# Loading Q weights ahead of K, wider Q/K matmuls, smaller weight pieces and an on-chip mask in a fused transformer block

## Chip, cores, metric

One core of a Trainium2 chip runs the whole program. The metric is device time in microseconds (us) of one execution; each kernel is run several times, and a profile is taken of one run. TensorE is called PE, VectorE DVE, ScalarE ACT, GpSimd POOL and SyncE SP, as in the profile; "PEld" is PE's weight load. The trace records the clock that PE was granted: 1.0 is full speed.

## The reference, cut to what matters

Two pre-normalized layers on 2,048 tokens of width 448: sliding, dilated attention (16 heads of 28, 8 keys per query at distance 2), then a mixer and an MLP.

```python
qkv = _layernorm(x) @ wqkv                    # 448 x 1344
idx = pos[:, None] - jnp.arange(8)[None] * 2  # 8 keys per token
attn = softmax(where(idx >= 0, q . k[idx] * scale, -1e9))
h = x + (attn . v[idx]) @ wo
# the second layer works on _layernorm(h):
# gelu(ln @ w1), shifted by 1 or 2 tokens, @ w2; then gelu(ln @ w3) @ w4   (w3: 448 x 1792)
```

## The kernel before: the parts concerned

Tokens are split by parity (index `a`), since the distance is 2: each parity is a sequence of 1,024, and `u` numbers its quarters of 256. HT holds the normalized activations, transposed. Its 448 rows do not fill 128-row tiles, so pairs of 64-row matmuls share PE's array ("r64"): in the trace of the changed kernel such a pair takes 216 ns with 512 columns, as one 128-row matmul of 512 columns does, and 109 with 256 (medians of the distances between starts).

The program is a list of operations with dependencies. A scheduler written in Python, inside the kernel file, replays that list with modelled durations and fixes the order of every engine before anything is compiled. Its constants are therefore part of the kernel, and so is a table of priorities (`rank`).

```python
LEAD = 600.0        # bulk DMAs may be issued this long before the queue runs dry (ns)
FETCH = 2900.0      # modelled time to fetch 256 PE instructions

def setup():
    load_x(0); load_x(1)
    wload("wqk", wst, A_wqkv[:, 0:2 * D], ("sp", "sp"))   # Q and K together, 4 transfers
    load_x(2); load_x(3)
    # ... constants; WARM = 36 dummy matmuls of 512 columns, lowest priority, wherever PE is free

def wqk_copies():                     # repacks the weights, 8 copies on ACT or DVE
    for c in range(4):
        for w in range(2): ...        # w = 0: Q, w = 1: K

def loads_b():
    dma("msk", msk[half[1], 1, :], msk[half[0], 1, :], 64 * 912, after=first)
    dve("tensor_copy", 280, out=msk[:, 0, :], in_=msk[:, 1, :])

def phase_QK(u):                      # u = 0..3
    for c in range(4):                # one tile: Q and K of 4 heads, 2 parities, 256 columns
        for w in range(2):
            for b in range(7):
                for a in range(2): ins.append(mm(... HT[r, b, 16+256*u : 16+256*u+256] ...))
        copy(QK[...], T(...), 1024)
# [cut: V, attention, WO, LN2, W1, W2, LN3, W3, W4]
```

## Time and profile before

| quantity | value | how to read it |
|---|---|---|
| three runs | 207.03, 207.33, 208.37 us | median 207.33 |
| profiled run | 209.0 us, span 207.2 | a slow run of this kernel; a second trace was taken later |
| PE busy | 92% of the span | PE is the bound, so its gaps and its clock matter |
| first Q/K matmul | 13.19 us | PE waits for weights until here |
| last matmul | 201.85 us | 5.4 us of stores follow |
| mean clock | 0.983 | two stretches of 3.41 us at half clock |

The prediction shows and explains the lines.

### The profile page before, as it was taken

How to read it: one execution, taken by the hardware profiler on the slowest of the kernel's cores; microseconds unless marked ns; L12 is line 12 of the kernel's file. 1: busy time of each engine (PE TensorE's matmuls, PEld its weight loads, DVE VectorE, ACT ScalarE, POOL GpSimd, SP SyncE). 2: the span in 40 equal slices, each digit the busy share in tenths (PEclk: the TensorE clock that was granted, in tenths of full speed). 3: DMA queues.
4: the chain of work that ended last, by engine and by line, in shares of the span. 5: the costliest groups of instructions: out<-in, count | busy, mean ns of one | idle time of the engine just before them, and what ended most of it. 6: DMA issues, size and time to landing. Idle time of an engine off the chain costs nothing.

```text
span 207.2 us, 7398 instructions
## 1 busy us (share of the span) xinstructions
PE 191.5 (92%) x3391; PEld 129.7 (63%) x3391; DVE 112.2 (54%) x261; ACT 101.8 (49%) x107; POOL 48.2 (23%) x90
## 2 busy tenths in 40 slices
PE   7859998996999999599999999999999999999990
PEld 2437765774756785446888555688895558855540
DVE  7569955442479908969990299990005920022221
ACT  2346699585349999950766900076672006700000
POOL 6311510000004500370850028770000730000000
PEclk9999999998899999979999999999999999999999
DMA  5996596654467500050252002561000231001111
GB/s 169 303 295 130 124 144 182 223 203 134 147 172 156 117 12 6 3 93 0 49 95 44 0 3 47 134 109 26 0 3 3 44 89 47 3 0 44 44 44 52
DMA packets 29610, 18.11 MB, mean 87 GB/s; under 512 B 21192, under 2 KB 28680, under 8 KB 29576
## 3 DMA queue, kind: packets, MB, share of 16 engines
q1 hardware_dynamic: 29576, 17.61, 34.1%
q8 instruction: 27, 0.44, 0.9%
q14 instruction: 7, 0.06, 0.1%
HBM read 10.67 MB, written 1.84 MB: 60 GB/s over the span
## 4 chain that ended last, share of the span: by engine, by line
PE 77%; DMA 7%; DVE 6%; ACT 3%; issue 3%; SPq 1%; POOL 1%
PE ps L1354 77%; DMA h<-in_A_wqkv_dram 4%; DMA HT<-ln 2%; DVE xin L1354 1%; ACT lnz L1354 1%; ACT pt L1354 1%; DVE pt L1354 1%; SPq L1354 1%; DVE st L1354 1%; DVE xb L1354 1%; DVE ln L1354 1%; POOL rstd L1354 1%; ACT QK L1354 0%; DVE arena L1354 0%; DVE mv L1354 0%
## 5 line engine op out<-in xcount | busy, mean ns | idle before, releaser
L1354 PE MATMUL ps<-HT,w_s 64*128 64x256 bf16 (+1 forms) x1064 | 56.0, 264 | 0.2 <-DMA HT<-ln 0.2
L1354 PEld LDWEIGHTS ps<-HT,w_s 64*128 64x128 bf16 x1064 | 49.5, 94 | 6.9 <-issue 1.1
L1354 DVE TENSOR_TENSOR xb<-ps,xb 128x448 bf16<-128x448 f32 (+1 forms) x24 | 18.4, 774 | 58.8 <-PE ps L1354 58.7
L1354 POOL TENSOR_SCALAR vtmp<-mv 128x2 f32<-128x2 f32 x32 | 6.2, 193 | 111.9 <-DVE mv L1354 110.5
L1354 ACT ACTIVATE arena<-ps 128x1024 bf16<-128x1024 f32 x14 | 14.3, 1024 | 36.1 <-PE ps L1354 36.1
L1354 PE MATMUL ps<-HT,arena 64*128 64x256 bf16 x448 | 28.1, 280 | 3.3 <-DVE arena L1354 2.3
L1354 ACT ACTIVATE QK<-ps 128x1024 bf16<-128x1024 f32 (+2 forms) x23 | 21.6, 948 | 14.2 <-PE ps L1354 14.1
L1354 PEld LDWEIGHTS ps<-HT,arena 64*128 64x128 bf16 x448 | 22.5, 98 | 8.6 <-issue 4.6
L1354 POOL TENSOR_TENSOR rstd<-vtmp,mhalf 128x2 f32<-128x2 f32 x32 | 22.5, 702 | 2.7
L1354 PE MATMUL ps<-w_s,h 128*128 128x448 bf16 x112 | 21.9, 352 | 0.2 <-issue 0.2
L1354 PE MATMUL ps<-w_s,arena 128*128 128x448 bf16 x112 | 21.5, 352 | 0.0
L1354 ACT ACTIVATE h<-ps 128x1024 bf16<-128x1024 f32 x14 | 14.3, 1024 | 12.5 <-PE ps L1354 12.5
L1354 DVE BATCH_NORM_STATS2 st<-xin 128x6 f32<-128x448 bf16 x32 | 18.4, 607 | 0.4 <-DMA xin<-in_A_x_dram 0.4
L1354 PEld LDWEIGHTS ps<-w_s,arena 128*128 128x128 bf16 x112 | 11.0, 98 | 10.2
L1354 PEld LDWEIGHTS ps<-w_s,h 128*128 128x128 bf16 x112 | 10.8, 98 | 10.3 <-issue 0.4
L1354 POOL TENSOR_TENSOR xb<-xb,xin 128x448 bf16<-128x448 bf16 x16 | 16.1, 1035 | 4.0 <-DVE ln L1354 4.0
L1354 ACT ACTIVATE pt<-ps 128x912 bf16<-128x912 f32 x18 | 15.7, 930 | 0.9 <-PE ps L1354 0.6
L1354 DVE TENSOR_SCALAR ln<-xin,mv,rstd 128x448 bf16<-128x448 bf16 x32 | 14.4, 496 | 2.4 <-POOL rstd L1354 2.1
L1354 DVE TENSOR_TENSOR QK<-ps,lnz 128x456 bf16<-128x456 f32 (+1 forms) x24 | 11.2, 505 | 6.1 <-PE ps L1354 5.9
L1354 PE MATMUL ps<-wv_s,HT 64*64 64x448 bf16 x252 | 14.2, 376 | 0.0
L1354 DVE TENSOR_TENSOR pt<-pt,msk 128x912 bf16<-128x912 bf16 x18 | 11.1, 628 | 4.7 <-ACT pt L1354 4.6
L1354 PE MATMUL ps<-wo_s,QK 128*128 128x448 bf16 x64 | 12.9, 358 | 0.0
(53 smaller groups left out, 167.8 us busy)
## 6 DMA issues: line engine op xcount, KB each, us to landing
w_s<-in_B_w_dram SPq DMA_DIRECT2D x6, 448.0 KB, 3.4
w_s<-in_B_w_dram SPq DMA_DIRECT2D x9, 224.0 KB, 2.9
xin<-in_A_x_dram SPq DMA_DIRECT2D x8, 224.0 KB, 7.9
out_dram<-xb SPq DMA_DIRECT2D x8, 224.0 KB, 1.9
h<-in_A_wqkv_dram SPq DMA_DIRECT2D x2, 672.0 KB, 6.0
wv_s<-in_A_wqkv_dram SPq DMA_DIRECT2D x2, 336.0 KB, 6.1
w_s<-in_B_w_dram SPq DMA_DIRECT2D x2, 336.0 KB, 3.4
wo_s<-in_A_wo_dram SPq DMA_DIRECT2D x4, 98.0 KB
```

The source lines that it names most:

```text
L1354: inst = getattr(eng, meth)(**kw)
```

## The change

The intent: let the Q part of the projection start while K's weights are still coming; shorten the list of PE instructions in the attention part; issue bulk weights in smaller pieces with less of a queue; keep the mask off the DMA queue. The scheduler's constants and priorities were fitted anew, so that the order of many operations differs.

```diff
-    LEAD = 600.0
+    LEAD = -300.0
-    FETCH = 2900.0
+    FETCH = 3400.0
-            fe[2] = at + self.FETCH + min(3600.0, 0.7 * max(0.0, qfree - at))
+            fe[2] = at + self.FETCH + min(1000.0, 0.5 * max(0.0, qfree - at))
 # [cut: modelled DMA rates 320 -> 300 and 200 -> 100]
-        wload("wqk", wst, A_wqkv[:, 0:2 * D], ("sp", "sp"))
+        for w in range(2):
+            wload("wqk%d" % w, wst[:, :, D * w:D * w + D], A_wqkv[:, D * w:D * w + D], ("sp", "sp"))
 # wqk_copies: the loops over c and w change places (all of Q first)
-        dma("msk", msk[half[1], 1, :], msk[half[0], 1, :], 64 * 912, after=first)
-        dve("tensor_copy", 280, out=msk[:, 0, :], in_=msk[:, 1, :])
+        for k in (1, 0):
+            dve("tensor_copy", 280, out=msk[half[1], k, :], in_=msk[half[0], 1, :])
+        dve("tensor_copy", 280, out=msk[half[0], 0, :], in_=msk[half[0], 1, :])
-        wload("w3", w3_s, B_w3, ..., each=True)
+        for k in range(2):
+            wload("w3_%d" % k, w3_s[:, :, 896 * k:896 * k + 896], B_w3[:, 896 * k:896 * k + 896], ..., each=True)
 # phase_QK(u) becomes phase_QK(u, nu) with 256*nu columns, and a tile holds Q or K, not both:
-    phase_QK(0) ... phase_QK(1) ... phase_QK(2) ... phase_QK(3)
+    phase_QK(0, 1) ... phase_QK(1, 1) ... phase_QK(2, 2)
 # [cut: a new table of priorities]
```

## The prediction

> **What bounds the kernel now.** I read first the busy shares, then the slices, then the chain that ended last, then TensorE's (PE's) timeline, and last the stretches where PE's clock or its idle time stood out.
>
> ```profile
> PE 191.5 (92%) x3391; PEld 129.7 (63%) x3391; DVE 112.2 (54%) x261; ACT 101.8 (49%) x107; POOL 48.2 (23%) x90
> PE   7859998996999999599999999999999999999990
> PEclk9999999998899999979999999999999999999999
> PE 77%; DMA 7%; DVE 6%; ACT 3%; issue 3%; SPq 1%; POOL 1%
> q8 instruction: 27, 0.44, 0.9%
> ```
>
> PE is 92% busy and makes 77% of the chain. It has three parts: until 13.2 us it waits for inputs, from 13.2 to 202.0 us it runs nearly without a gap, and a 5 us tail stores the last rows. So only four things can shorten the span: an earlier start, less PE work, fewer PE gaps, fewer slow-clock stretches. The start, from the chain in order of time:
>
> ```profile
> 2.71 0.55 SPq L1354
> 3.27 0.04 issue
> 3.31 9.02 DMA h<-in_A_wqkv_dram
> 12.33 0.02 issue
> 12.36 0.70 DVE arena L1354 x2
> 13.05 0.14 issue
> 13.19 1.71 PE ps L1354 x28
> ```
>
> The Q and K weights land together at 12.33; two repacking copies follow, then the first Q/K matmul at 13.19. The other operand, HT, was ready at 10.50 (ACT's two copies: from 8.53, 1.97 us). The gaps, from PE's timeline:
>
> ```profile
> 36.31 0.28 PE L1354 MATMUL ps<-pt,vt 64*32 64x57 bf16 x23 [0.81 <-issue]
> 40.44 1.25 PE L1354 MATMUL ps<-HT,arena 64*128 64x256 bf16 x19 [0.29 <-issue]
> 49.48 0.30 PE L1354 MATMUL ps<-pt,vt 64*32 64x57 bf16 x28 [1.49 <-issue]
> ...
> 83.61 0.23 PE L1354 MATMUL ps<-pt,vt 64*32 64x57 bf16 x11 [0.40 <-issue]
> ...
> 85.72 0.31 PE L1354 MATMUL ps<-QK 28*64 28x57 bf16 x13 [0.63 <-ACT lnz L1354]
> 87.17 0.34 PE L1354 MATMUL ps<-QK 28*64 28x57 bf16 x19 [1.15 <-issue]
> ```
>
> "issue" means that PE waited for nothing the profile knows, and always in the middle of a run of identical small matmuls. Counting matmuls up to each: 604 before the first, 731 before the second, 986 before the third: spacings of 128 or (nearly) a multiple of it. Each matmul is a load and a multiply, so 128 are 256 instructions. These are waits for instruction fetch: 0.44 MB in 27 transfers is 16 KB each, 256 instructions of 64 bytes. They sum to 0.81 + 0.29 + 1.49 + 0.40 + 1.15 = 4.14 us. And busy time and clock by stretch:
>
> ```profile
> 36.50:50.00 13.50, 11.13 (x416) 8.46 (x395) 5.92 (x9) 10.13 (x11) 0.00 (x0) 1.00 0.59 199
> 50.00:60.00 10.00, 10.00 (x164) 6.96 (x161) 4.24 (x6) 3.89 (x5) 0.00 (x0) 0.83 0.45 127
> 76.00:88.00 12.00, 9.78 (x462) 6.65 (x460) 9.58 (x19) 11.19 (x14) 1.57 (x4) 0.98 0.01 4
> 88.00:97.00 9.00, 9.00 (x66) 4.17 (x56) 7.03 (x13) 2.70 (x3) 4.20 (x5) 0.84 0.31 54
> ```
>
> (Columns: stretch, length, busy of PE, PEld, DVE, ACT, POOL, PE clock, DMA share, GB/s.) Each stretch with fetch gaps is followed by one with a mean clock of 0.83 or 0.84. The trace's clock record has exactly two half-rate pieces in the body, 49.94 to 53.36 and 87.49 to 90.90, right behind the 1.49 and 1.15 us gaps. 84 QK matmuls there take 6.42 us instead of 4.76. Half of 3.41 us is lost in each: 3.4 us in all.
>
> [...] PE was about half busy, not idle, in the window ahead of each (1.85 us in the first). [...] here a block took 3.56 us boundary to boundary with idle queues (83.61 to 87.17) and 4.13 with weights loading (36.31 to 40.44).
>
> **The change part by part.** The instruction order of the changed kernel can be listed without running it, and I cut both into blocks of 128 matmuls (after the first 93).
>
> *Start.* Q comes as 784 KB ahead of K's 784 KB, each in four transfers instead of four for both. In the old kernel 1,568 KB landed between about 3.5 us (x there, DVE begins at 3.42) and 12.33. Half of that time is 4.4 us, so Q by 7.9; rows of 896 bytes instead of 1,792 make twice the packets, so I take 8.6 to 9.4 (an estimate). HT is then the later operand: on DVE the first Q copy (0.38) stands ahead of the second pair of normalizations, and ACT does a Q copy (0.85) before the HT copies. From Q at 9.0: copy to 9.4, normalize 0.97 to 10.4, transposes 0.56, HT copy 0.92, so PE starts near 11.9 to 12.0, against 13.19. The mask copies on DVE (3 x 0.25 us and two memsets) lie in front of Q's landing and are free; the mask's DMA of 57 KB goes. K (estimated 12.5 to 13.5) has 56 Q matmuls, 3.3 us, to hide behind. Part of the gain could be lost at the next tokens' transposes, since their statistics now stand behind K's copies on DVE. Net: -1.0.
>
> *PE work.* 224 matmuls of 256 columns become 112 of 512. Today 28 of them need 1.63 us start to start (31.74 to 33.37), 58 ns each; the weights' 308 ran at 55.2. With 512 columns the fixed part is paid half as often: about 108 each. 224 x 57.5 - 112 x 107.5 = 0.84. -0.8. The columns streamed do not change, so no more is to be had. ACT and DVE still evacuate 16 tiles of 1,024 elements.
>
> *Fetch.* 112 matmuls fewer is 0.875 of a block, so about one fetch fewer, and the order is reshuffled. Pure work per block, at durations from the timeline (57-column 10 ns, 448-column 49 or 189, warm-up fillers 216), in the critical part:
> old, from matmul 349: 4.7, 2.6, 3.8, 3.6, 2.8, 5.3 us; later (76 to 88 us): 2.9, 2.9, 1.5
> new, from matmul 349: 3.7, 3.4, 3.1, 3.2, 4.5, 8.3 us; later: 3.8, 2.6, 7.2
> [...] With 3.9 us under load the new early blocks lose 0.2 + 0.5 + 0.8 + 0.7 = 2.2, and the 2.6 block about 1.0 at 3.6: 3.2 against 4.14. [...] the worst old case, 1.49, fell among the 448 KB pieces. -1.0, with 1.2 either way.
>
> *Clock.* The 1.5 us block and its neighbours are gone, and no two new blocks are so short that half a window stands empty. I give each slow window two chances in three of vanishing: 2 x 1.7 x 0.65 = -2.2.
>
> *New waits.* Between the second W2 group and the first W3 matmul the new order has 10.6 us of PE work; in the old trace the path from W2's end (82.4) to the landed transposes (93.7) took 11.3. +0.3 to +0.5. ACT's table loads fall from six to four, 2 x 1.28 us, but late, where ACT waits for PE: nothing. The tail is unchanged.
>
> Sum: -1.0 - 0.8 - 1.0 - 2.2 + 0.4 = -4.6, and 207.3 becomes 202.7.
>
> **Rivals.** (a) The early start is eaten: PE arrives sooner at attention but is held by ACT's softmax chain or the later transposes, and only work and clock pay. For: ACT is busy 9.10 of 9.50 us in 27 to 36.5, and 11.19 of 12 in 76 to 88. Against: data waits there are about 1 us in all and ACT is not full in between. Then about 204. (b) Fetch stays the bound: evenly short blocks of 3.1 to 3.4 us all stall if contention makes the period 4.5 to 5, as happened once. That is 4 x 1.3 us, no gain, perhaps one slow window left: 205 to 206. For: the bulk loads move into the same stretch. Against: smaller pieces. (c) All goes well: no slow window, fetch waits of 1.5 us, start at 11.5: -1.6 - 0.8 - 2.6 - 3.4 = -8.4, so 199.
>
> **Range and chances.** Clock and fetch each carry an uncertainty of a good microsecond and are linked[...]. I take 199.8 to 205.6. The 2% line is at 203.2, half a microsecond above my value, so it is little better than even: 0.57 faster, 0.41 within 2%, 0.02 slower, since nothing in the change adds PE work.
>
> **What would show it.** Right: the first Q/K matmul near 12 us; 112 matmuls of 512 columns at 107 to 110 ns; "issue" gaps that sum to about 3 us, none over 1.2; no slice under 9 in the clock row of the body; the rest of PE's stream unchanged. Wrong: a start at 13 or later (Q not ahead, or HT held by the copies), a new DMA wait ahead of W3, slow windows still there, or an ACT or DVE wait of over 1 us in attention.

## The result, and the profile after

The changed kernel took 200.88 us (median of 4 runs, 200.41 to 201.24) against 207.85 (4 runs, 207.03 to 208.87) in the same rounds. The ratio is 0.9661, interval 0.9608 to 0.9715: faster. Ratios here are the record's: fast runs of one kernel over fast runs of the other in the same rounds. They are not quite the ratio of the medians, nor of the means over all the runs listed. The time lies in the predicted range, on its fast side.

First the page of the changed kernel: engine totals, two rows of the slices, the chain by engine.

```profile
PE 186.8 (94%) x3275; PEld 123.0 (62%) x3279; DVE 111.0 (56%) x262; ACT 99.3 (50%) x106; POOL 48.3 (24%) x90
PE   7599999899999999999899999999999999999990
PEclk9999999999999999999999999999999999999999
PE 70%; DVE 12%; ACT 9%; POOL 3%; DMA 2%; issue 2%; POOLq 0%
```

The clock row has no digit under 9 any more, and the only slices of PE under 8 are the first two and the last. DMA fell from 7% to 2% of the chain: the weights no longer release the start. Next, PE's timeline of the same run, four lines: the first Q/K matmuls, the one fetch gap left, the new wait ahead of the later W1 matmuls, and the end.

```profile
11.35 6.29 PE L1360 MATMUL ps<-HT,arena 64*128 64x256 bf16 x112
...
38.88 0.82 PE L1360 MATMUL ps<-HT,arena 64*128 64x512 bf16 x5 [0.82 <-issue]
...
98.33 3.23 PE L1360 MATMUL ps<-HT,w_s 64*128 64x256 bf16 x56 [0.50 <-DMA HT<-ln]
...
193.46 0.16 PE L1360 MATMUL ps<-ones,fbit 128*1 128x1 bf16 x1
```

This trace has three more "issue" gaps, 0.16, 0.25 and 0.16 us, in the attention part. They are not waits: beside each the list of instructions has one more warm-up matmul of 216 ns than the trace records (this trace has 3,275 matmuls, those of e0_changed and e0c, of the same kernel, 3,279). Such a gap has to be counted against the program before it is read as a stall.

The same four stretches as before, with the same columns:

```profile
36.50:50.00 13.50, 12.43 (x378) 6.28 (x378) 6.92 (x11) 11.40 (x14) 0.00 (x0) 1.00 0.32 88
50.00:60.00 10.00, 10.00 (x180) 5.38 (x182) 9.27 (x21) 6.97 (x9) 2.64 (x6) 1.00 0.51 117
76.00:88.00 12.00, 11.09 (x311) 6.27 (x310) 11.97 (x24) 6.12 (x9) 6.13 (x8) 1.00 0.51 123
88.00:97.00 9.00, 8.96 (x197) 8.88 (x196) 8.95 (x28) 7.88 (x8) 3.72 (x9) 1.00 0.60 84
```

PE is busy 1.3 us more in each of the first and third stretch, and the clock is 1.00 in all four. (These are the same times, not the same work, since the order differs.)

The first profile of the kernel before was a slow run, so it must not be held against a fast one. A second trace of it, fast (206.94 us, span 205.2; run e8_before below), has these waits of PE:

```profile
12.41 5.07 PE L1354 MATMUL ps<-HT,arena 64*128 64x256 bf16 x84 [1.62 <-DVE arena L1354]
...
40.29 1.25 PE L1354 MATMUL ps<-HT,arena 64*128 64x256 bf16 x19 [0.84 <-issue]
...
49.33 0.30 PE L1354 MATMUL ps<-pt,vt 64*32 64x57 bf16 x28 [1.49 <-issue]
...
81.63 0.23 PE L1354 MATMUL ps<-pt,vt 64*32 64x57 bf16 x11 [0.37 <-issue]
...
84.91 0.34 PE L1354 MATMUL ps<-QK 28*64 28x57 bf16 x19 [0.87 <-issue]
```

Start 12.41, fetch gaps 0.84 + 1.49 + 0.37 + 0.87 = 3.57 us, one slow clock window in the body (85.67 to 89.08). Against a fast trace of the changed kernel (run e0_changed, span 198.6, start 11.44, last matmul 193.24, fetch gap 0.64) the 6.6 us between the spans come out so: start 1.0; fetch 2.9; half of one slow window 1.7 (in the first trace the 84 matmuls under one took 6.42 us, in e8_before the same 84 at full clock 4.76); the remaining 1.0 is data waits (1.6 us in the old stream, 1.4 in the new one), the tail and what is too small to name.

### The profile page after: what moved, and what is told of

It reads as the page before. It is cut to its first block, busy times and chain, and to the rows that moved or that the text cites. A ratio compares the mean times of both kernels' runs of the same rounds, so it can differ in the third digit from the quotient of the medians.

```text
span 199.1 us, 7188 instructions
## 1 busy us (share of the span) xinstructions
PE 186.8 (94%) x3275; PEld 123.0 (62%) x3279; DVE 111.0 (56%) x262; ACT 99.3 (50%) x106; POOL 48.3 (24%) x90
## 4 chain that ended last, share of the span: by engine, by line
PE 70%; DVE 12%; ACT 9%; POOL 3%; DMA 2%; issue 2%; POOLq 0%
PE ps L1360 70%; ACT QK L1360 3%; ACT pt L1360 3%; DVE st L1360 2%; DVE ln L1360 2%; DVE xin L1360 2%; DVE QK L1360 2%; ACT lnz L1360 2%; DMA HT<-ln 2%; DVE xb L1360 2%; DVE pt L1360 1%; ACT L1356 1%; POOL wo_s L1360 1%; POOL rstd L1360 1%; POOL msk L1360 1%
## 5 line engine op out<-in xcount | busy, mean ns | idle before, releaser
L1360 PEld LDWEIGHTS ps<-HT,w_s 64*128 64x128 bf16 x1064 | 50.6, 94 | 6.2 <-issue 1.1
L1360 ACT ACTIVATE QK<-ps 128x1024 bf16<-128x1024 f32 (+2 forms) x24 | 22.5, 951 | 15.1 <-PE ps L1360 15.1
L1360 PE MATMUL ps<-HT,arena 64*128 64x256 bf16 (+1 forms) x336 | 26.5, 305 | 1.2 <-issue 0.8
L1360 PEld LDWEIGHTS ps<-HT,arena 64*128 64x128 bf16 x336 | 15.6, 94 | 9.5 <-issue 1.9
L1360 PEld LDWEIGHTS ps<-w_s,arena 128*128 128x128 bf16 x112 | 10.9, 98 | 10.2
L1360 POOL TENSOR_TENSOR xb<-xb,xin 128x448 bf16<-128x448 bf16 x16 | 16.6, 1068 | 0.2 <-DVE ln L1360 0.2
L1360 PE MATMUL ps<-w_s,QK 112*128 112x448 bf16 x64 | 13.0, 353 | 0.0
L1360 PE MATMUL ps<-wv_s,HT 64*64 64x448 bf16 x252 | 12.7, 351 | 0.1
```

Source lines behind the costliest of these rows:

```text
L1360: inst = getattr(eng, meth)(**kw)
```

## The experiments

For each experiment on the changed kernel, its order was computed first, and the edit was made on the finished order. So an edit moves nothing else. Differences are of means, in us, against the changed kernel on the same chip; the intervals of the ratios to the kernel before are 0.35 to 1.2% to either side, since that kernel itself scatters by up to 2.5%. The changed kernel scatters by up to 0.7%. Worked out from the runs listed, the 95% intervals of the differences are about 1.0 us to either side for e1, 0.9 for e1c and e3, 1.3 for e2, 1.2 for e9 and 0.4 for e5c. So the +0.80 of e3 alone is not clear of noise.

| run | edit | median us | ratio to before | against the changed kernel |
|---|---|---|---|---|
| e0_changed, e0c | none | 200.42, 200.70 | 0.9688, 0.9731 | (200.61 and 200.69 mean) |
| e1_one_load, e1c | Q and K in one load | 201.40, 201.43 | 0.9717, 0.9784 | +0.95, +1.03 |
| e2_cols256 | 256 columns again | 202.09 | 0.9750 | +1.50 |
| e3_big_pieces | w3 in 8 pieces again | 201.32 | 0.9723 | +0.80 |
| e9_order_only | all three undone | 203.73 | 0.9884 | +3.5 (+3.2 without the profiled run) |
| e7_small_fillers | 12 fillers shortened | 201.46 | 0.9699 | other chip |
| e5_ht_first, e5c | HT first, mask copies later | 199.43, 199.50 | 0.9634, 0.9674 | -1.23 (e5c) |
| e8_before | the kernel before | 207.08 | 0.9985 | |
| e6_before_shift64 | before, 64 tiny matmuls more | 207.61 | 0.9998 | |

**The yardstick.** Two sets of the unchanged new kernel.

> The changed kernel once more, so that the next three have it on their own chip. All theories: 200.4 to 201.3 us, no slow clock window in the body, one instruction-fetch gap of about 0.8 us near 38 us.

> The changed kernel as the yardstick for the next three on one chip: 200.3 to 201.2 us, gap of 0.6 to 0.9 us near 38 us.

Both came out as expected: means of 200.61 and 200.69, no slow window in the body of either trace. e0c's fetch gap was 1.01 us, a little more than expected.

**One load for Q and K.**

```diff
     q, k = S.qk_loads[:4], S.qk_loads[4:]
+    for o, kw in zip(q, whole_width): o.ins = [("dma_start", kw)]   # Q's transfers fetch Q and K
+    # K's transfers are dropped; normalizations and HT copies go ahead of the repacking on DVE and ACT
```

> The changed kernel with Q and K weights in one set of four transfers again, and the order on DVE and ACT that suits it (normalizations and HT copies ahead of the repacking); everything else in the same order. Theory (start passes on in full): first Q/K matmul back at 13.0 to 13.4 us instead of 11.35, time 1.6 to 2.0 us over the changed kernel, 202.4 to 203.0. Rival (early start is eaten by later waits): within 0.4 us of the changed kernel.

> One load for Q and K again, once more, as its first set of runs lay 1.0 us over the changed kernel while its trace said 2.0 at the start. Theory (full passing, the load's landing varies between runs): first Q/K matmul between 12.4 and 13.5, time over the changed kernel by what the trace shows of the start, within 0.5 us. Rival (half of it is absorbed by later waits): 1.0 us over whatever the start says.

The first set was 0.95 us over the changed kernel, against an expected 1.6 to 2.0. Its trace started Q/K at 13.46, 2.0 later than the yardstick's, but that was the slowest of its six runs (202.67; the others 200.57 to 202.22). So the set was repeated: +1.03, now with a trace of a more usual run (201.22, median 201.43).

```profile
12.49 6.29 PE L1411 MATMUL ps<-HT,arena 64*128 64x256 bf16 x112 [1.09 <-DVE arena L1411]
```

12.49 is 0.97 later than e0c's 11.52, and the mean time 1.03 more. The traces show where the start goes: PE reaches the fetch gap near 38 us 2.00 us later than the yardstick in e1 and 1.02 in e1c, so up to there the start passes on in full. From there the gap itself differs between runs (0.64 to 1.01 us in the yardsticks), and the last matmul comes 2.28 and 0.44 us later. What had misled me was the landing of the single load, which differs between runs by about a microsecond (11.34 to 12.33, and Q/K starts at 12.41 to 13.46, in the six traces that have it).

**256 columns again.**

```diff
-  mm(out[:, 0:512], lhsT, rhs[:, 0:512], start, stop)
+  mm(out[:, 0:256], lhsT, rhs[:, 0:256], start, False); mm(out[:, 256:512], lhsT, rhs[:, 256:512], False, stop)
```

> The changed kernel with each 512-column Q/K matmul cut into two of 256 columns, all else in the same order: 112 matmuls more. Theory A (fewer instructions to fetch): blocks of 128 matmuls of 2.6, 2.8, 2.7, 2.9 and 2.6 us appear, fetch gaps sum to 3 to 5 us instead of 0.8, 203.5 to 206.5 us, perhaps with a slow window. Theory B (fixed cost per matmul, as I predicted it): 0.8 us more and no new gap, 201.7. Theory C (only the new order matters): 201.0.

1.50 us more. The fetch gaps of its trace:

```profile
39.34 1.27 PE L1400 MATMUL ps<-HT,arena 64*128 64x256 bf16 x19 [1.33 <-issue]
...
47.01 0.30 PE L1400 MATMUL ps<-pt,vt 64*32 64x57 bf16 x28 [0.99 <-issue]
...
82.36 0.58 PE L1400 MATMUL ps<-QK 28*64 28x57 bf16 x47 [0.56 <-issue]
```

2.88 us against 0.64: new gaps, as theory A had it, though smaller than its 3 to 5, and the time fell short of its 203.5. (Q/K also started 0.51 us later in this trace than in e0_changed, which the edit does not explain.) The matmuls themselves decide against theory B. The longest run of them in each kernel:

```profile
47.24 3.23 PE L1400 MATMUL ps<-HT,arena 64*128 64x256 bf16 x56
```

```profile
45.62 3.20 PE L1360 MATMUL ps<-HT,arena 64*128 64x512 bf16 x28
```

56 of 256 columns take 3.23 us, 28 of 512 take 3.20. That is 0.03 us for 28 of the wide ones, about 0.1 us for all 112. From one pair of 64-row matmuls to the next it is 109 ns with 256 columns and 216 with 512 (medians in e0_changed), so a wide pair saves 2 ns and the 56 wide pairs 0.1 us. The wide matmuls pay off because they are fewer instructions, hardly because they run faster.

**Larger weight pieces.** Each pair of w3 transfers is fetched as one, in the place of its first.

```diff
-  16 transfers: 12 of 224 KB, 4 of 112 KB (column halves of w3, one half after the other)
+  8 transfers: 6 of 448 KB, 2 of 224 KB (all columns)
```

> The changed kernel with w3 in 8 transfers of the old sizes (448 and 112 KB) instead of 16, each in the place of the first of its pair. Theory (a fetch waits behind bulk transfers, smaller pieces shorten that): gaps in 30 to 60 us grow by 0.5 to 1.5 us in sum, 201.4 to 202.4. Rival (sizes don't matter, the pacing or the order does): within 0.3 us of the changed kernel.

(The 112 KB in the expectation is a slip: the small pieces have 224 KB, as in the diff.) 0.80 us more, inside the theory's range, but not for its reason, and with an interval that reaches zero. The gap near 38 us was 0.86, no more than in the yardsticks (0.64 to 1.01). A new wait stands at the first W3 matmul:

```profile
89.53 2.69 PE L1416 MATMUL ps<-HT,w_s 64*128 64x256 bf16 x46 [1.07 <-DMA w_s<-in_B_w_dram]
```

With all columns in every piece, the first W3 group waits for the last piece; in the changed kernel it needs the first column half alone, and no such wait exists (that half had landed by 69.05 us in e0_changed; here the last piece landed at 89.49). The wait of 0.54 at the later W1 is gone in exchange, so 0.53 us of it remains. So cutting w3 by columns helps the start of W3 in this order. That piece size matters to instruction fetch is not shown by this run; the size was changed without changing the pacing, and pacing by itself was not tried.

**The order alone.**

> The changed kernel's order and on-chip mask alone: one load for Q and K, 256 columns, w3 in 8 pieces. Theory (parts add): 1.0 + 1.5 + 0.8 over the changed kernel, 203.9 us (203.2 to 204.6), so that the new order is worth some 3 us against 207.4, with fetch gaps of 2.5 to 3.5 us still there, but no gap over 1.4 and at most one slow clock window in the body. Rival (order is worth nothing, the parts do it all): 206.5 to 208, two slow windows.

All three edits at once: 203.73 median; the parts add up (0.99 + 1.50 + 0.80 = 3.3, measured 3.5 over all six runs, which are all fast, or 3.2 without the profiled one). Against the kernel before, 0.9884 remains (0.9828 to 0.9940; within 2%, so classed as the same, but clear of 1): the new order and the on-chip mask are worth some 2.4 us (0.0116 of 206; the interval says 1.2 to 3.5, and all six runs listed give 2.0). "Order" here includes the pacing of the loads and the tiles that hold Q or K alone, which this run keeps too. Its fetch gaps sum to 1.82 us (1.56 + 0.26), less than the 2.5 to 3.5 expected. How this order still suffers is seen at 40.91, in its slowest run, the profiled one:

```profile
40.91 1.97 PE L1447 MATMUL ps<-HT,arena 64*128 64x256 bf16 x19 [1.56 <-issue]
42.81 0.94 PE L1447 MATMUL ps<-QK 28*64 28x57 bf16 x64
43.68 2.20 PE L1447 MATMUL ps<-HT,arena 64*128 64x256 bf16 x28
```

The gap is larger than I had allowed (1.56, not under 1.4). The clock record goes to half from 41.32 to 44.73, right behind it: 19 matmuls need 1.97 us there, 1.27 in e2_cols256, which had the same instructions, a gap of 1.33 and no slow window.

**Are the gaps instruction fetch?** The kernel before, untouched, and with 64 matmuls of 32 columns added where PE waits for the weights anyway:

```diff
+    last_warm_up.ins += [matmul(out[:, 0:32], same weights, rhs[:, 0:32])] * 64
```

> The kernel before once more, because its first profile fell in a slow run (209.0 us, its others 207.0 to 208.4). All theories: 206.5 to 208 us. Theory (fetch gaps follow from the instruction count): the issue gaps stand at the same matmuls (about 604, 731, 986, 1880, 2010) and sum to 3 to 4.5 us; one or two slow clock windows in the body. Rival (gaps are chance of that run): other places.

> The kernel before with 64 matmuls of 32 columns added while TensorE waits for the Q/K weights, nothing else. Theory (instruction fetch in blocks of 128 matmuls): every gap moves 64 matmuls towards the start of the stream. Old gaps at 604, 731, 986 are gone; new ones near 411 and 667 (inside runs of 57-column Q/K matmuls), near 923, and 1819 and 1947 of the old count. Blocks of 2.6, 2.1, 3.1, 2.8 and 1.6 us against a period of 3.6 to 4.1: gaps of about 1.2, 1.7, 0.7, 0.8 and 1.9, 6.3 in sum instead of 4.1, time 1 to 3 us over the kernel before. Rival (gaps belong to certain data or buffers): same places, same time.

Untouched, four of the five old gaps stand at the same matmuls; the one at 604 was absent. With 64 more, all old places are clean (the profiled run is a slow one, 207.73 us, so its gaps are read for their places first), and:

```profile
38.16 0.38 PE L1387 MATMUL ps<-QK 28*64 28x57 bf16 x23 [1.47 <-issue]
...
47.66 1.27 PE L1387 MATMUL ps<-HT,arena 64*128 64x256 bf16 x20 [0.78 <-issue]
...
85.00 0.60 PE L1387 MATMUL ps<-pt,vt 64*32 64x57 bf16 x51 [1.00 <-issue]
```

The first is in the middle of a run of Q/K products, after the 668th matmul of the old count (expected near 667), the second after the 922nd (923), the third 13 records into the run in which 1947 lies. Counted from the start of the stream with the 64 included, they stand at 732, 986 and 2007, where the untouched kernel has gaps at 731, 986 and 2007 (a trace misses a few matmuls); the changed kernel's one gap is at 731 too. So the gaps belong to instruction number, not to data.

That they are fetch can be seen in the DMA records of the same traces, which list each 16 KB instruction transfer: 27 in the first trace, where PE executes 6,782 instructions, and 26 in the trace of the result, with 6,554. In all 14 traces, 25 "issue" gaps of 0.29 us or more stand before 90 us, and each ends 1.07 to 1.53 us after such a transfer has landed. With idle queues (83.6 us in the first trace of the kernel before; DMA share 0.01 from 76 to 88) the transfer of the next block began 1.1 us after PE had entered a block, took 0.96, and the new block started 1.45 later, 3.56 us from boundary to boundary. Where weights were loading it began later: ahead of the 1.49 us gap, 2.8 us after PE had entered the block (at 44.4 us; DMA share 0.70 from 44 to 48), and 2.7 in e8_before. At the same matmul of e0_changed it was 1.2, with less bulk traffic (DMA share 0.13 from 40 to 44), and of e3_big_pieces 1.5. So the fetch began sooner in that stretch; the pacing of the loads is the likely reason, but it was not tested alone.

The sizes were overrated: three of five expected gaps, 3.25 us instead of 6.3, and the time did not change (0.9998, 0.9957 to 1.0040). Those of 411 and 1819 did not show. The count gives the places where a gap can stand; adding the work of a block from durations says poorly whether one comes and how long it is. And the changed kernel is not far from the limit: in e0_changed four block boundaries in a row (30.7, 34.6, 38.7 and 42.5 us) are crossed 1.3 to 1.6 us after a transfer landed, as at the gaps.

**What the fillers do.**

```diff
   for the 12 warm-up matmuls behind the first Q/K matmul:
-  mm(out[:, 0:512], flat[:, 0:128], flat[:, 128:640])
+  mm(out[:, 0:32],  flat[:, 0:128], flat[:, 128:160])
```

> The changed kernel with the 12 warm-up matmuls inside the attention part (512 columns, 216 ns each) cut to 32 columns, same number of instructions. Theory (they fill time in which TensorE would wait anyway): within 0.4 us, other gaps appear in their place; if a window gets too empty, a slow clock window and up to 1.7 us more. Rival (they stand in the way): up to 2.2 us less.

Its four runs spread from 199.80 to 203.44, the slowest of them (of the slow state) with a mean clock of 0.980, while the changed kernel stays within 200.1 to 201.5. The profiled run (201.67) shows small data waits in place of the fillers, no gap over 0.3 us up to there, and then a slow window from 29.24 to 32.65. Columns as before:

```profile
26.00:29.20 3.20, 2.52 (x144) 1.87 (x138) 1.32 (x3) 2.70 (x5) 0.00 (x0) 1.00 1.29 145
29.20:32.70 3.50, 3.44 (x36) 2.06 (x36) 1.90 (x3) 1.89 (x4) 0.00 (x0) 0.51 0.25 62
```

PE looks busy for 2.52 of 3.20 us before the clock drops; much of that is products of 28 rows and 57 columns. In the changed kernel (the trace of the result) PE is busy for 2.96 us of the same stretch, and no slow window follows. So the fillers may be no waste, but it is one trace; of the other two fast runs none lists a clock under 0.995. As the set is small and on another chip than the yardstick, its mean is not compared.

**Can the start be taken further?** The chain of waits of the changed kernel shows what its start hangs on:

```profile
4.41 0.27 DVE msk L1360
...
4.71 1.15 DVE st L1360 x2
5.87 0.22 DVE mv L1360 x2
...
6.12 0.27 DVE msk L1360
...
8.26 0.30 DVE arena L1360
```

Mask copies on DVE stand inside the statistics of the first tokens (and DVE waits 0.51 us for POOL ahead of the first one), and the repacking of Q stands ahead of the second normalization. So:

```diff
+  move the 3 mask copies and 2 memsets behind the normalizations of the fourth token group (DVE)
+  move both first normalizations (DVE) and both HT copies (ACT) ahead of the repacking of Q
```

> The changed kernel with the mask copies on DVE moved behind the fourth group of normalizations, and the first two groups of normalizations and their HT copies put ahead of the repacking of Q. Theory (start passes on in full): first Q/K matmul at 9.8 to 10.2 us instead of 11.4, time 1.2 to 1.6 us under the changed kernel. Rival (the rest of the start is eaten): within 0.4 us.

> The version with HT ahead of the repacking and the mask copies later, now beside the changed kernel on one chip. Theory (start passes on in full): 1.0 to 1.5 us under the changed kernel, first Q/K matmul near 10.2. Rival (no gain in the mean): within 0.3 us.

```profile
10.30 6.41 PE L1392 MATMUL ps<-HT,arena 64*128 64x256 bf16 x112
```

10.30 instead of 11.52, and 1.23 us less (six runs of each on one chip: 198.98 to 199.85 against 200.38 to 200.94). The start passes on in full in this direction too. (The first set, on another chip than the yardstick, started at 10.28, just outside its 9.8 to 10.2, and took 199.43.) Which of the two moves brings how much was not separated. This version, 199.50 us, beats both kernels, and its outputs are correct.

**What a slow window costs.** The runs of the kernel before in three of the sessions, 49, list mean clock and time. A straight line through the 35 fast ones gives 0.7 us more for each 0.01 less of clock (correlation -0.45); through all 49 it gives 1.2 (-0.60), but that mixes states, while the fast ones alone leave out the slowest runs by definition. One window of 3.41 us at half clock is 0.008 of the mean, so by these lines 0.6 to 1.0 us and not the full 1.7. The mean clocks of the two kernels' fast runs beside each other (chip of e0c) are 0.985 and 0.997: by the lines 0.9 to 1.5 us. It is a correlation only, and the tail, which runs at half clock in part (from 206.95 us of the first trace, 4.9 us after the end of PE's last matmul) and costs nothing there, counts in the mean.

## Why the prediction was right

It said 202.7, 199.8 to 205.6, and faster by over 2% with a chance of 0.57. It came out at 200.88 by the mechanism that it named, an earlier start, fewer fetch gaps and no slow windows; two terms of the sum were mis-sized.

- **Start, -1.0: right.** e1 gives 0.95 and 1.03. The path to it was off in two details. Q and K landed sooner than 8.6 to 9.4 and 12.5 to 13.5 (the first copy of Q on ACT could go at 8.02, that of K on DVE at 10.56), though the packets did double (up to 13 us the first trace has 1,434 packets of 1,792 bytes and 642 of 896, the trace of the result 539 and 2,641), and "the mask copies ... are free" was wrong: they are on the chain of waits. The fear that part is lost at the next tokens' transposes did not come true: up to the fetch gap near 38 us the start passes on in full in e1, e1c and e5c.
- **PE work, -0.8: wrong.** The term was "224 x 57.5 - 112 x 107.5 = 0.84". e2's trace gives about 0.1. The 58 ns came from one group of 28 with its edges, and the 107.5 was an estimate: a pair of 64-row matmuls takes 109 ns with 256 columns, 216 with 512, 2 ns less than two narrow pairs.
- **Fetch, -1.0: right in kind, too small.** Gaps went from 4.14 and 3.57 us in the two old traces to 0.64 to 1.01 in three new ones, about 2.9 us. The step that failed is "the new early blocks lose 0.2 + 0.5 + 0.8 + 0.7 = 2.2, and the 2.6 block about 1.0": one gap came instead of five. The step takes each block's work off a period of 3.9 us (the last block's off 3.6), between the measured 3.56 and 4.13, and counts what is missing as a gap: an estimate. Pure block durations overrated the gaps here as in e6 (6.3 us expected, 3.25 measured). The mechanism itself, blocks of 128 matmuls, was confirmed by e6 and by the instruction transfers in the traces, and e2 shows that the smaller count does much of it.
- **Smaller pieces against long fetches: no effect shown.** e3 found a cost of 0.80 for large pieces, not clear of noise, and its trace shows it as a late first W3. That a fetch began later beside bulk traffic is seen in the traces (2.8 us to its beginning against 1.1 with idle queues); what the pieces' size has to do with it is not.
- **Clock, -2.2: right in kind, the size is not settled.** No slow window stood in the body of any of three traces of the changed kernel, against two and one before. The time lost at half rate fell by 2.5 us (0.997 - 0.985, times 207, tail included), and e8's single window alone is 1.7 us of its trace; the correlation makes 0.9 to 1.5 of it. "Two chances in three of vanishing" was borne out, the full 1.7 us for each perhaps not. Part of it may be luck of where a gap falls, but that was not shown: e8 had the same 1.49 us gap as the first trace, and no slow window behind it. In the first trace all changes of the clock record lie whole multiples of 3.413 us apart (both slow windows last one such step, and their starts are 11 apart). Counted back from e8's later slow window in such steps, one ends at 48.12, inside that gap, and PE was busy for 2.56 and 2.21 us of the two steps that share it, against 1.85 and 1.64 of the 3.41 us ahead of the slow windows of the first trace. No busy share at which the clock drops is shown: in e7 it dropped behind a stretch with 2.52 of 3.20 us.
- **New waits, +0.4: about 0.** The wait foreseen ahead of W3 came at the later W1 (0.42 to 0.54 us), but the old kernel had waits of that size elsewhere.

The two mis-sized terms partly cancel: 0.7 us too much gain from the work, 1.9 too little from fetch. Rival (a), the start eaten by attention, is refuted by e5c, and e1 and e1c point the same way; rival (b), fetch stays the bound, by the traces. With the sizes measured, the terms sum to 4.9 to 5.5 us (clock by the correlation) or 6.5 (clock by the time at half rate); measured are 7.0 (the result), 6.6 (beside e0_changed) and 5.6 (beside e0c). So up to 2 us has no term. What stays open: which of the many moves of the new order bring its 2.4 us, and how much of that is the mask or the pacing of the loads.

## What to carry to other kernels

Where one engine runs thousands of very short instructions (here 6,782 on PE in 207 us), count instructions in the blocks that the gaps show (here 256) and look where a block holds less work than a fetch takes (here 3.56 us from boundary to boundary with idle queues); fewer and larger instructions paid there even though each takes as long as what it replaces (1.50 us in e2). Summed durations did not say how long the waits would be (6.3 us expected in e6, 3.25 measured), so look at the instruction transfers in the trace. A gap of a microsecond on PE was followed by a slow clock in some runs (1.49 and 1.15 us in the first trace, 1.56 in e9) and not in others (1.49 in e8, 1.33 in e2), so fillers in such a stretch may be worth more than they take. An input that releases the first matmul passed on in full here, where PE is the bound (0.97 us later and 1.03 us more in e1c, 1.22 sooner and 1.23 less in e5c), so follow the chain of waits to the first matmul and move everything off it that is needed only later.
